# A banked Strassen-type MLP behind pooled attention and an FFT: one PSUM bank per product, a shared ring of four, and moved front-end stages

## The chip, the cores and the metric

The kernel runs on one core of a Trainium2 chip. The metric is device time in microseconds (us), the median of the runs shown. Engines are named as the profile names them: PE is TensorE's matmul, PEld its weight load, DVE is VectorE, ACT ScalarE, POOL GpSimd, SP the engine that issues most DMAs.

## The reference

Eight sequences of 576 tokens pass an attention whose keys and values are averaged over groups of eight tokens, then a two-dimensional FFT mix, a layer norm and a two-layer MLP of width 512 to 2048 to 512 with ReLU. Cut to what is computed:

```python
k_p = k.reshape(B, H, Sp, pool, D).mean(axis=3)
v_p = v.reshape(B, H, Sp, pool, D).mean(axis=3)
scores = scale * np.matmul(q, k_p.transpose(0, 1, 3, 2))
attn = np.exp(scores - np.max(scores, axis=-1, keepdims=True))
attn = attn / (np.sum(attn, axis=-1, keepdims=True) + 1e-09)
x = np.matmul(attn, v_p)               # heads side by side: (8, 576, 512)
X = np.fft.fft(np.fft.fft(x, axis=1), axis=2)
u = x + np.real(X)
un = (u - np.mean(u, -1)) / np.sqrt(np.var(u, -1) + 1e-06)
out = u + np.maximum(un @ w_ch1, 0.0) @ w_ch2
```

## The kernel before

The work has two halves that run side by side. The **front end** `fe(b)` (line 298) makes the normalised rows of sequence b: attention scores (tiles psS, line 394), transposes (psT, psV, psR), values (psX), the cosine and sine transforms (psA, psB, psQ, psP), the mean (psM), the variance (psVar), Newton steps for the reciprocal root, and last the operands of the MLP (`operands`, line 678). It is a generator of some 31 stages. The **MLP** `fast()` (line 848) is a second generator that works in nine blocks of 512 tokens. Block 0 is done by `plain()` (line 825) with ordinary products while the weights are still being split into high and low parts (`prep_w`, line 180; two MLP weight matrices in 32 pieces). Blocks 1 to 8 use a Strassen-type scheme: for each pair of hidden chunks (j = 0 to 7) seven products of 256 columns each, six matmuls a product (line 897), combined by seven DVE instructions (line 857, and the copy of line 900) into two hidden chunks, which pass ReLU on ACT (line 865), a rounded copy (line 866) and a remainder on POOL (line 867). The second layer, `gemm2` (line 789), comes in thirds of four matmuls of 512 columns (line 799) that are placed between the products of the next pair: the order of products and thirds is written in `MID`, `FIRST` and `LAST`.

Each product and each third ends in a `yield`, which counts one place. `advance(pos)` (line 950) runs a front-end stage when the place reaches its number in the table `AT` (`AT1` for sequence 1), counted from the start of the block before; 104 places are one block. `AHEAD` (line 52) says how many weight pieces are split ahead of the places. From place 92 on PE's instructions stand in the order in which the program writes them; DVE, ACT, POOL and the DMA queue are ordered by a scheduler.

PSUM has eight banks of 512 columns. The four accumulators of the second layer hold one each (tags acc0 to acc3). The front end takes turns on two banks (tag "fe", line 282). The products take turns on four **halves** of two banks (lines 850 and 851), so that two products that follow each other often lie in one bank. In the built program a product that starts in a bank waits until the addition that reads the other half has ended; the wait stands at about every second product.

Of the kernel before, what the change touches and what calls it, by code (L numbers as in the profile page):

```python
# [8 lines left out]
F32 = mybir.dt.float32  # L9
# [7 lines left out]
PSUM = bass.MemoryType.PSUM  # L17
# [5 lines left out]
P = 128  # L23
# [6 lines left out]
BLK = 512  # L30
# [18 lines left out]
UE = [1, 1, 0]  # L49
UL = [3, 3, 2]  # L50

AHEAD, WBUFS, LOOK = 7, 12, 9

RES = [0, 2, 5, 7, 9, 12, 14]

UNITS0, UNITS, MANUAL, TAIL = 90, 104, 92, (2, 8, 14, 20, 26)
AT = [-32, -22, -19, -9, -6, -4, -1, 13, 14, 16, 18, 25, 27, 27, 37, 40, 44, 47, 51, 51, 55, 58, 61, 67, 67, 80, 80, 81, 82, 83, 104]
AT1 = [-1] * 7 + [2 + 3.5 * n for n in range(17)] + [78, 79, 80, 82, 83, 84, 96]
E0, O0, E1, O1 = 0, 1, 2, 3

HB = BLK // 2
# [26 lines left out]
def raw(ap):  # L88
    return ap.bitcast(F32)
# [3 lines left out]
def tile_kernel(ctx: ExitStack, tc: tile.TileContext, qt, kt, vm, vr, w1, w2, cad, cbd, mkd, out):  # L93
    nc = tc.nc
    cp = ctx.enter_context(tc.tile_pool(name="cp", bufs=1))
    wk = ctx.enter_context(tc.tile_pool(name="wk", bufs=1))
    pp = ctx.enter_context(tc.tile_pool(name="pp", bufs=1, space=PSUM))
    dp = ctx.enter_context(tc.tile_pool(name="dp", bufs=1, space=bass.MemoryType.DRAM))
    wide = w1.dtype != F32
# [139 lines left out]
    for k in range(1, NBLK + 1):  # L239
        for j in range(NFC // 2):  # L240
# [4 lines left out]
            for x in MID if k < NBLK and j else FIRST:  # L245
                if x != "g" and k < NBLK:
                    items.append(("a", k, j, PROD[x][0]))
                elif x == "g":
                    f = 2 * prev[1] + g // 3
# [20 lines left out]
    def use(x):  # L270
        flow[0] = max(flow[0], where[x])
        return tiles.pop(x)


    turn, behind = [0], {}

    def bank(b, name, late=False):
        tag = "fe"
        if b == 0 and not late:
            tag = ["g1", "acc0", "g1", "acc1", "acc2", "acc3"][turn[0] % 6]  # L280
            turn[0] += 1
        return pp.tile([P, 512], F32, tag=tag, bufs=2 if tag in ("fe", "g1") else 1, name=name)

    def keep_busy(ins, n):

# [500 lines left out]
    def accs(k):  # L786
        return [pp.tile([P, 512], F32, tag=f"acc{e}", name=f"acc{k}_{e}") for e in range(4)]

    def gemm2(acc, f, hh, hl, got):
        order = [(x, e) for x in range(3) for e in range(4)]  # L790
        if f == NFC - 1:
            order = [(x, e) for e in range(4) for x in range(3)]
        w = []
        for n, (x, e) in enumerate(order):
            if n in (4, 8):
                yield
            w = w or [t.rearrange("p (c m) -> p c m", m=P) for t in got()]
            a, h = ((w[0], hh), (w[1], hh), (w[0], hl))[x]
            nc.tensor.matmul(acc[e], lhsT=a[:, e], rhs=h, start=(f == 0 and x == 0), stop=(f == NFC - 1 and x == 2))  # L799
        yield  # L800

    def weights2(k, f):
        def got():
            if k == 0:
                return highs.pop((1, f)), lows.pop((1, f))
            wh = w2h[:, RES.index(f)] if f in RES else use(("h", k, f))
            return wh, use(("l", k, f))
        return got
# [16 lines left out]
    def plain():  # L825
        xh, xl = [flat(t)[:, 0:2048].rearrange("p (c n) -> p c n", c=4) for t in un(0)]
        acc = accs(0)
        prev = None
        for f in range(NFC):
            ah, al = [t.rearrange("p (c m) -> p c m", m=P) for t in (highs.pop((0, f)), lows.pop((0, f)))]  # L830
            ps = pp.tile([P, 512], F32, tag="g1", bufs=2, name=f"g1_{f}")
            n = 0
            for w, x in ((ah, xh), (ah, xl), (al, xh)):
                for c, ti in enumerate((E0, O0, E1, O1)):
                    nc.tensor.matmul(ps, lhsT=w[:, c], rhs=x[:, ti], start=(n == 0), stop=(n == 11))
                    n += 1
                if n < 12:
                    yield
            hs = [wk.tile([P, BLK], F32R, tag=t, bufs=3, name=t) for t in ("hh", "hl")]
            nc.scalar.activation(hs[0], ps, AF.Relu)  # L840
            nc.vector.scalar_tensor_tensor(out=hs[1], in0=ps, scalar=0.0, in1=raw(hs[0]), op0=ALU.max, op1=ALU.subtract)  # L841
            yield
            if prev:
                yield from prev
            prev = gemm2(acc, f, *hs, weights2(0, f))
        return acc, [prev]

    def fast():
        acc, todo = yield from plain()
        gs = [pp.tile([P, 512], F32, tag="g1", bufs=2, name=f"x{i}") for i in range(2)]  # L850
        banks = [t[:, HB * i:HB * i + HB] for t in gs for i in range(2)]
        s24, c0, c2, s1 = [sx[:, BLK * i:BLK * i + BLK] for i in range(4)]
        s1 = s1[:, 0:HB]
        count = 0

        def add(o, x, y):
            nc.vector.tensor_tensor(out=o, in0=x, in1=y, op=ALU.add)  # L857

        def wide(x):
            return x.rearrange("p (h n) -> p h n", h=2)  # L860

        def relu(c):
            h = wk.tile([P, BLK], F32R, tag="hh", bufs=3, name="hh")
            l = wk.tile([P, BLK], F32R, tag="hl", bufs=3, name="hl")
            nc.scalar.activation(c, c, AF.Relu)  # L865
            nc.scalar.copy(out=h, in_=c)  # L866
            nc.gpsimd.tensor_tensor(out=l, in0=c, in1=raw(h), op=ALU.subtract)  # L867
            return h, l

        def step():  # L870
            while todo:
                if next(todo[0], 0) is None:
                    return True
                todo.pop(0)
            return False

        for k in range(1, NBLK):
            bh, bl = un(k)
            todo_of = acc
            for j in range(NFC // 2):  # L880
                last = k == NBLK - 1 and j == NFC // 2 - 1
                for x in FIRST if j == 0 else LAST if last else MID:
                    if x == "g":
                        if step():
                            yield
                        elif todo_of is not None:
                            evict(k - 1, todo_of)
                            todo_of = None
                        continue
                    ps = banks[count % 4]  # L890
                    count += 1
                    a, c = PROD[x]
                    w = use(("a", k, j, a)).rearrange("p (q c m) -> p q c m", q=2, m=P)
                    n = 0
                    for q, t in ((0, bh), (0, bl), (1, bh)):
                        for i in range(2):
                            nc.tensor.matmul(ps, lhsT=w[:, q, i], rhs=t[:, 2 * c + i], start=(n == 0), stop=(n == 5))  # L897
                            n += 1
                    if x == 1:
                        nc.vector.tensor_copy(out=s1, in_=ps)  # L900
                    elif x == 6:
                        add(s24[:, 0:HB], ps, s1)
                    elif x == 2:
                        add(c0[:, 0:HB], ps, s1)
                    elif x == 5:
                        add(s24[:, HB:BLK], ps, s24[:, 0:HB])
                    elif x == 3:
                        add(c0[:, HB:BLK], ps, s24[:, HB:BLK])
                        hs0 = relu(c0)
                    elif x == 7:  # L910
                        add(wide(c2), ps.unsqueeze(1).broadcast_to([P, 2, HB]), wide(s24))
                    elif x == 4:
                        add(c2[:, 0:HB], ps, c2[:, 0:HB])
                        hs1 = relu(c2)
                    yield
                while step():
                    yield
                if j == 0:
                    if todo_of is not None:
                        evict(k - 1, todo_of)  # L920
                    acc = accs(k)
                todo += [gemm2(acc, 2 * j + m, *hs, weights2(k, 2 * j + m)) for m, hs in enumerate((hs0, hs1))]
        while step():
            yield
        evict(NBLK - 1, acc)
# [21 lines left out]
    def start(k):  # L947
        return UNITS0 + UNITS * (k - 1) if k else 0

    def advance(pos):  # L950
        for c in sorted(run):
            r = run[c]
            while r[1] < len(AT) and pos >= (AT1 if c == 1 else AT)[r[1]] + start(c - 1):
                r[1] = len(AT) - 1 if next(r[0], None) == "ln" else r[1] + 1
        c = max(run) + 1
        if c < B and pos + 1 >= AT[0] + start(c - 1):
            run[c] = [fe(c), 0]
# [122 lines left out]
```

## Time and profile before

| what | value |
|---|---|
| runs, median (lowest to highest) | 1236.73 us (1235.58 to 1240.16) |
| profiled execution, its own time | 1243.98 us |
| its span, first to last instruction | 1242.2 us |
| PE busy | 1066.7 us (86%) |
| DVE busy | 775.0 us (62%) |
| ACT busy, POOL busy | 569.1 us, 569.6 us (46% each) |
| mean granted TensorE clock | 0.946 |

The profiled execution is one run; its span leaves out 1.8 us of its time. Busy shares are means over stretches with different limits: up to about 100 us there is the front end of sequence 0, to about 275 us the plain block, to about 1064 us the blocks that share the core with a front end, and from there on blocks alone. A row of PE with a time in square brackets gives the idle time before it and what ended it.

### The profile page before, as it was taken

To read this page: it belongs to the slowest core of one execution; us is meant where nothing else is said; L and a number is where in the kernel's file an instruction comes from. 1 tells how busy PE (TensorE), PEld (TensorE's weight loads), DVE (VectorE), ACT (ScalarE), POOL (GpSimd) and SP (SyncE) were. 2 spreads that over 40 slices of the span, in tenths; PEclk is the share of its full clock that TensorE was granted. 3 is DMA by queue.
4 is the path that set the end of the run, shared out by engine and by line. 5 is a ranking of instruction groups with operands and counts; after the bars stand their busy time and mean duration, and the time that the engine had idled before them with its cause. 6 is when DMAs were issued, how large, how long until landed. Compare 5 with 4: busy or idle time off the path is not lost.

```text
span 1242.2 us, 19110 instructions
## 1 busy us (share of the span) xinstructions
PE 1066.7 (86%) x6118; PEld 902.7 (73%) x6118; DVE 775.0 (62%) x1479; ACT 569.1 (46%) x1698; POOL 569.6 (46%) x531
## 2 busy tenths in 40 slices
PE   7778778868898889788978899798988998999998
PEld 5556456747786778677867787687867887888886
DVE  7586776885468656865577647865686567422322
ACT  6577554655327632664255534663266323222221
POOL 4375595654544555437444543555433244222221
PEclk9878889878999989998999999998999999999999
DMA  8538584756665766566665666576655666777874
GB/s 285 177 109 271 165 264 133 237 168 205 190 204 166 235 197 194 174 206 199 191 190 171 218 193 210 157 223 203 191 168 182 187 186 205 251 247 241 263 244 135
DMA packets 142755, 249.57 MB, mean 201 GB/s; under 512 B 15808, under 2 KB 36288, under 8 KB 142400
## 3 DMA queue, kind: packets, MB, share of 16 engines
q1 hardware_dynamic: 142368, 245.69, 63.7%
q0 software_dynamic: 288, 2.66, 0.6%
q8 instruction: 49, 0.80, 0.3%
q14 instruction: 50, 0.41, 0.1%
HBM read 217.63 MB, written 30.67 MB: 200 GB/s over the span
## 4 chain that ended last, share of the span: by engine, by line
PE 48%; DVE 26%; issue 8%; ACT 7%; DMA 4%; POOL 3%; SPq 0%; DVEq 0%; ACTq 0%; POOLq 0%
PE acc L799 20%; PE x L897 17%; DVE sx L857 4%; ACT t L403 2%; DVE X L690 2%; DVE unl L687 2%; PE psX L474 2%; DMA sx<-in_w 2%; DVE mx L396 2%; DVE U L821 1%; PE psP L632 1%; DVE X L779 1%; DVE rw L376 1%; DVE lf L725 1%; PE psB L615 1%
## 5 line engine op out<-in xcount | busy, mean ns | idle before, releaser
L897 PE MATMUL x<-unh,w1op 128*128 128x256 f32 x1792 | 372.2, 292 | 94.4 <-DVE sx L857 74.5
L897 PEld LDWEIGHTS x<-unh,w1op 128*128 128x128 f32 x1792 | 296.8, 194 | 151.8 <-DVE sx L857 103.7
L857 DVE TENSOR_TENSOR sx<-x,sx 128x256 f32<-128x256 f32 (+1 forms) x384 | 178.2, 466 | 212.0 <-PE x L897 209.9
L867 POOL TENSOR_TENSOR hl<-sx,hh 128x512 fp32r<-128x512 f32 x128 | 173.7, 1358 | 295.5 <-ACT hh L866 231.5
L865 ACT ACTIVATE sx<-sx 128x512 f32<-128x512 f32 x128 | 81.3, 635 | 328.8 <-DVE sx L857 328.5
L897 PE MATMUL x<-unl,w1op 128*128 128x256 f32 x896 | 180.7, 284 | 2.2 <-DVE unl L687 2.2
L799 PE MATMUL acc<-hh,w2low 128*128 128x512 f32 x576 | 167.1, 405 | 0.0
L897 PEld LDWEIGHTS x<-unl,w1op 128*128 128x128 f32 x896 | 141.1, 195 | 2.7 <-DVE unl L687 2.7
L799 PEld LDWEIGHTS acc<-hh,w2low 128*128 128x128 f32 x576 | 103.5, 194 | 16.3
L799 PE MATMUL acc<-hh,w2high 128*128 128x512 f32 x324 | 98.6, 414 | 3.6 <-ACT hh L840 2.6
L403 ACT ACTIVATE t<-psS,mx 128x72 f32<-128x72 f32 x280 | 86.2, 334 | 23.3 <-DVE mx L399 23.0
L799 PE MATMUL acc<-hl,w2high 128*128 128x512 f32 x324 | 94.0, 398 | 0.0
L411 POOL TENSOR_TENSOR t<-t,sm 128x720 f32<-128x720 f32 x32 | 49.5, 1547 | 75.3 <-DVE sm L410 41.1
L866 ACT CAST hh<-sx 128x512 fp32r<-128x512 f32 x128 | 79.7, 622 | 3.4
L799 PE MATMUL acc<-hh,w2h 128*128 128x512 f32 x252 | 75.1, 423 | 3.6 <-ACT hh L840 3.6
L799 PE MATMUL acc<-hl,w2h 128*128 128x512 f32 x252 | 74.5, 419 | 2.0 <-DVE hl L841 2.0
L799 PEld LDWEIGHTS acc<-hh,w2high 128*128 128x128 f32 x324 | 58.8, 198 | 13.2 <-ACT hh L840 3.2
L394 PE MATMUL psS<-kpb,q 128*128 128x144 f32 x280 | 47.9, 310 | 22.1 <-ACT t L403 11.3
L329 POOL TENSOR_TENSOR k<-k 128x288 f32<-128x288 f32 (+1 forms) x56 | 38.4, 685 | 61.5 <-DMA k<-in_kt 59.0
L799 PEld LDWEIGHTS acc<-hl,w2high 128*128 128x128 f32 x324 | 56.8, 190 | 8.8 <-issue 0.4
L394 PEld LDWEIGHTS psS<-kpb,q 128*128 128x128 f32 x280 | 40.1, 199 | 31.6 <-ACT t L403 16.2
L403 ACT ACTIVATION_READ_ACCUMULATOR t<-psS,mx 128x1 f32 x280 | 61.5, 220 | 0.0
(267 smaller groups left out, 1979.3 us busy)
## 6 DMA issues: line engine op xcount, KB each, us to landing
w1op<-w1s SPq DMA_DIRECT2D x448, 256.0 KB, 3.2
w2low<-w2l SPq DMA_DIRECT2D x128, 256.0 KB, 3.1
w2high<-w2d SPq DMA_DIRECT2D x72, 256.0 KB, 3.4
U<-in_w SPq DMA_DIRECT2D x16, 512.0 KB, 4.2
sx<-in_w SPq DMA_DIRECT2D x16, 512.0 KB, 4.5
q<-in_qt SPq DMA_DIRECT2D x28, 288.0 KB, 2.9
k<-in_kt SPq DMA_DIRECT2D x28, 288.0 KB, 3.3
v<-in_vm SPq DMA_DIRECT2D x28, 256.0 KB, 3.0
```

The lines of the kernel that those rows point to most:

```text
L329: nc.gpsimd.tensor_tensor(out=out if n == 1 else src[:, :, 0:n], in0=src[:, :, 0] if n == 1 else src[:, :, 0:n], in1=src[:, :, 1] if n == ...
L394: nc.tensor.matmul(ps[:, c * W2J:(c + 1) * W2J], lhsT=q[:, r0:r0 + P], rhs=kpb[g % 2], start=True, stop=True)
L396: nc.vector.tensor_reduce(out=mx[:, c0:c0 + n], in_=pv, op=ALU.max, axis=AX.X, negate=b in SM)
L403: nc.scalar.activation(t[:, c0 + c, h], pv[:, c, h], AF.Exp, scale=1.0 / 64.0, bias=mx[x], accum_out=sm[x])
L411: ins = nc.gpsimd.tensor_tensor(out=t, in0=t, in1=sm.unsqueeze(3).broadcast_to([P, 5, 2, J]), op=ALU.mult)
L474: behind["X", b] = nc.tensor.matmul(ps, lhsT=w, rhs=a, start=(i == 0), stop=(i == len(mm) - 1))
L799: nc.tensor.matmul(acc[e], lhsT=a[:, e], rhs=h, start=(f == 0 and x == 0), stop=(f == NFC - 1 and x == 2))
L857: nc.vector.tensor_tensor(out=o, in0=x, in1=y, op=ALU.add)
L865: nc.scalar.activation(c, c, AF.Relu)
L866: nc.scalar.copy(out=h, in_=c)
L867: nc.gpsimd.tensor_tensor(out=l, in0=c, in1=raw(h), op=ALU.subtract)
L897: nc.tensor.matmul(ps, lhsT=w[:, q, i], rhs=t[:, 2 * c + i], start=(n == 0), stop=(n == 5))
```

## The change

The products no longer use halves of two banks. When `plain()` has ended, the pool that held "g1" and "fe" (two banks each) is closed and a new one with four banks of one tag is opened; every product and every later front-end tile takes the next of these four in turn (`shared`). The additions of a product are issued with priority, so that the scheduler of DVE takes one first when it is ready. The tables are new: stages move by 1 to 12 places, sequence 2 has a table of its own (`AT2`, the early stages alone differ from `AT`), in `AT1` the last stages go from 78, 79, 80, 82, 83, 84 to 64, 69, 71, 73, 74, 75, and three more weight pieces are split ahead.

```diff
-AHEAD, WBUFS, LOOK = 7, 12, 9
+AHEAD, WBUFS, LOOK = 10, 12, 9
...
-AT = [-32, -22, -19, -9, -6, -4, -1, 13, 14, 16, 18, 25, 27, 27, 37, 40, 44, 47, 51, 51, 55, 58, 61, 67, 67, 80, 80, 81, 82, 83, 104]
+AT = [-36, -28, -23, -5, -3, -1, 2, 13, 14, 16, 18, 25, 27, 28, 38, 41, 44, 47, 51, 52, 55, 57, 60, 66, 66, 76, 76, 77, 78, 79, 104]
+AT2 = [-36, -28, -23, -13, -11, -9, -6] + AT[7:]
...
     def bank(b, name, late=False):
-        tag = "fe"
         if b == 0 and not late:
-            tag = ["g1", "acc0", "g1", "acc1", "acc2", "acc3"][turn[0] % 6]
             turn[0] += 1
-        return pp.tile([P, 512], F32, tag=tag, bufs=2 if tag in ("fe", "g1") else 1, name=name)
+            tag = ("g1", "acc0", "g1", "acc1", "acc2", "acc3")[(turn[0] - 1) % 6]
+            if tag != "g1":
+                return pp.tile([P, 512], F32, tag=tag, name=name)
+            return shared("g1", name)
+        return shared("fe", name)
...
+    def shared(kind, name):
+
+        if len(pools) == 2:
+            return pools[1].tile([P, 512], F32, tag=kind, bufs=2, name=name)
+        return pools[0].tile([P, 512], F32, tag="b", bufs=4, name=name)
...
-        gs = [pp.tile([P, 512], F32, tag="g1", bufs=2, name=f"x{i}") for i in range(2)]
-        banks = [t[:, HB * i:HB * i + HB] for t in gs for i in range(2)]
...
+        pools[0].__exit__(None, None, None)
+        pools[:] = [ctx.enter_context(banks())]
         for k in range(1, NBLK):
...
-                    ps = banks[count % 4]
-                    count += 1
+                    ps = shared("g1", "x")[:, 0:HB]
...
-                    if x == 1:
-                        nc.vector.tensor_copy(out=s1, in_=ps)
+                    with tc.high_priority():
+                        if x == 1:
+                            nc.vector.tensor_copy(out=s1, in_=ps)
...
-            while r[1] < len(AT) and pos >= (AT1 if c == 1 else AT)[r[1]] + start(c - 1):
+            while r[1] < len(AT) and pos >= (AT1 if c == 1 else AT2 if c == 2 else AT)[r[1]] + start(c - 1):
```

**PE, the score tiles of sequence 6 (psS6), in the late part of a block.** x is a product's tile, acc4 an accumulator of the second layer (the first of four matmuls of a third is shown, and the first row of three of a product). Before:

```order
L739 MATMUL psVar5_7503<-qhl_7496,avg_75 128x288
...
L394 MATMUL psS6_3_0_7536<-kpb1_77,q6_3_7411 128x144 x3
L394 MATMUL psS6_3_3_7548<-kpb1_77,q6_3_7411 128x144 x2
L897 MATMUL x0_2244<-unh4_5089,w1op_7439 128x256 x2
...
L799 MATMUL acc4_0_6638<-hl_7405,w2high_7369 128x512
...
L897 MATMUL x1_2245<-unh4_5089,w1op_7448 128x256 x2
...
L394 MATMUL psS6_2_0_7629<-kpb0_76,q6_2_7425 128x144 x3
L394 MATMUL psS6_2_3_7641<-kpb0_76,q6_2_7425 128x144 x2
```

Now:

```order
L754 MATMUL psVar5_7688<-qhl_7681,avg_75 128x288
L409 MATMUL psS6_3_0_7700<-kpb1_77,q6_3_7591 128x144 x3
L409 MATMUL psS6_3_3_7712<-kpb1_77,q6_3_7591 128x144 x2
L814 MATMUL acc4_0_6818<-hl_7526,w2h_69 128x512
...
L911 MATMUL x_7760<-unh4_5179,w1op_7569 128x256 x2
...
L814 MATMUL acc4_0_6818<-hh_7641,w2high_7579 128x512
...
L911 MATMUL x_7795<-unh4_5179,w1op_7627 128x256 x2
...
L911 MATMUL x_7805<-unh4_5179,w1op_7646 128x256 x2
...
L409 MATMUL psS6_2_0_7816<-kpb0_76,q6_2_7605 128x144 x3
L409 MATMUL psS6_2_3_7828<-kpb0_76,q6_2_7605 128x144 x2
```

Between the two pairs of score tiles two products and one third stood before; now it is three products and two thirds. In turn of the four banks, product x_7805 takes the bank of psS6_3_0 and psS6_2_0 that of psS6_3_3.

**DVE, the end of the values of sequence 5 (psX5_1) and the split of tmpE.** The rows of line 857 (now 870) are additions of products; lines 376 and 367 (391 and 382) prepare the value weights. Before:

```order
L857 TENSOR_TENSOR sx<-x_2245,sx 128x256
L485 TENSOR_TENSOR U<-psX_1_6881,U 128x288
L565 TENSOR_TENSOR tmpE<-U 128x2x287
L376 SCALAR_TENSOR_TENSOR rw_79<-vt,mk,rw_79 32x63
L376 SCALAR_TENSOR_TENSOR rw_79<-vt,mk,rw_79 32x1
L367 SCALAR_TENSOR_TENSOR wlo<-vs,mk,wh 128x64
L857 TENSOR_TENSOR sx<-x_2244,sx 128x256
L367 SCALAR_TENSOR_TENSOR wlo<-vs,mk,wh 128x63
L367 SCALAR_TENSOR_TENSOR wlo<-vs,mk,wh 128x1
L559 TENSOR_TENSOR f<-tmpE,f 128x580
L857 TENSOR_TENSOR sx<-x_2244,sx 128x256
```

Now:

```order
L870 TENSOR_TENSOR sx<-x,sx 128x256
L500 TENSOR_TENSOR U<-psX_1_7069,U 128x288
L580 TENSOR_TENSOR tmpE<-U 128x2x287
L391 SCALAR_TENSOR_TENSOR rw_79<-vt,mk,rw_79 32x63
L391 SCALAR_TENSOR_TENSOR rw_79<-vt,mk,rw_79 32x1
L382 SCALAR_TENSOR_TENSOR wlo<-vs,mk,wh 128x64
L870 TENSOR_TENSOR sx<-x,sx 128x256
L382 SCALAR_TENSOR_TENSOR wlo<-vs,mk,wh 128x63
L382 SCALAR_TENSOR_TENSOR wlo<-vs,mk,wh 128x1
L870 TENSOR_TENSOR sx<-x,sx 128x256
L574 TENSOR_TENSOR f<-tmpE,f 128x580
```

Here the second addition now stands ahead of the remainder of tmpE; the first keeps its place behind the five front-end instructions.

## Rows read from the trace of the kernel before

**Rows 1.** Page, span and busy time (share) of the engines.

```profile
span 1242.2 us, 19110 instructions
...
PE 1066.7 (86%) x6118; PEld 902.7 (73%) x6118; DVE 775.0 (62%) x1479; ACT 569.1 (46%) x1698; POOL 569.6 (46%) x531
```

**Rows 2.** Waits of PE, 277 to 1064 us: us in total, times, longest.

```profile
PE x L897 <- DVE sx L857: 67.5, 53, 4.6
PE x L897 <- DVE sx L900: 12.4, 11, 3.2
PE psS L394 <- ACT t L403: 9.7, 13, 1.0
PE psS L394 <- DVE R L460: 4.8, 7, 1.1
```

**Rows 3.** Timeline, 700 to 712 us: start, us, engine, line, operation, tiles, [idle before].

```profile
703.84 1.09 PE L799 MATMUL acc<-hh,w2low 128*128 128x512 f32 x4
...
706.38 2.25 DVE L376 SCALAR_TENSOR_TENSOR rw<-vt,mk,rw 32x63 fp32r<-32x63 f32 x2
...
709.02 0.41 DVE L857 TENSOR_TENSOR sx<-x,sx 128x256 f32<-128x256 f32 x1
...
709.49 0.80 PE L897 MATMUL x<-unh,w1op 128*128 128x256 f32 x2 [4.56 <-DVE sx L857]
```

**Rows 4.** Timeline, 1088 to 1094 us, blocks without a front end.

```profile
1088.80 0.42 DVE L857 TENSOR_TENSOR sx<-x,sx 128x256 f32<-128x256 f32 x1 [1.19 <-PE x L897]
...
1089.28 0.50 PE L897 MATMUL x<-unh,w1op 128*128 128x256 f32 x2 [0.52 <-DVE sx L857]
...
1091.01 0.40 PE L897 MATMUL x<-unh,w1op 128*128 128x256 f32 x2
...
1091.69 1.09 PE L799 MATMUL acc<-hl,w2high 128*128 128x512 f32 x4
...
1092.62 0.39 PE L897 MATMUL x<-unh,w1op 128*128 128x256 f32 x2
```

**Rows 5.** Windows: length, busy us of five engines, granted clock, DMA share, GB/s.

```profile
706.00:710.00 4.00, 0.51 (x2) 0.51 (x3) 3.94 (x7) 0.68 (x1) 3.80 (x5) 0.84 0.68 205
710.00:714.00 4.00, 4.00 (x17) 3.61 (x16) 1.60 (x4) 0.00 (x0) 1.76 (x3) 0.50 0.29 82
718.00:852.00 134.00, 115.82 (x717) 100.83 (x716) 89.88 (x175) 64.11 (x209) 63.61 (x61) 0.96 0.63 195
1064.00:1242.20 178.20, 166.31 (x1014) 144.69 (x1014) 54.64 (x118) 38.86 (x62) 40.65 (x31) 1.00 0.74 233
245.00:290.00 45.00, 30.62 (x127) 24.65 (x126) 35.02 (x73) 21.38 (x78) 19.96 (x15) 0.73 0.58 189
200.00:245.00 45.00, 35.66 (x161) 27.66 (x160) 40.48 (x59) 27.18 (x80) 32.22 (x27) 0.92 0.58 185
```

**Rows 6.** Timeline, 768 to 776 us: score tiles on PE, their exponentials on ACT.

```profile
768.17 1.39 PE L394 MATMUL psS<-kpb,q 128*128 128x144 f32 x10
...
772.42 0.34 ACT L403 ACTIVATE t<-psS,mx 128x72 f32<-128x72 f32 x1
...
772.90 1.00 PE L394 MATMUL psS<-kpb,q 128*128 128x144 f32 x6 [1.03 <-ACT t L403]
...
774.17 0.36 ACT L403 ACTIVATE t<-psS,mx 128x72 f32<-128x72 f32 x1
...
774.68 0.76 PE L394 MATMUL psS<-kpb,q 128*128 128x144 f32 x4 [0.78 <-ACT t L403]
```

**Rows 7.** Waits of PE, 1064 to 1243 us.

```profile
PE x L897 <- DVE sx L857: 7.0, 12, 0.9
```

**Rows 8.** Groups by line, 0 to 277 us: count | busy us, mean ns.

```profile
L198 DVE SCALAR_TENSOR_TENSOR wdl<-sx,wdl 128x512 int32<-128x512 int32 x10 | 9.8, 975 | 2.9 <-ACT wdl L195 2.5
...
L230 DVE TENSOR_TENSOR wdh<-wdh 128x256 f32<-128x256 f32 x8 | 7.7, 960 | 0.1
```

More of the change, by code (lines that the diff above doesn't have):

```diff
@@ L50 @@
 UL = [3, 3, 2]
-AHEAD, WBUFS, LOOK = 7, 12, 9
+AHEAD, WBUFS, LOOK = 10, 12, 9
 RES = [0, 2, 5, 7, 9, 12, 14]
 UNITS0, UNITS, MANUAL, TAIL = 90, 104, 92, (2, 8, 14, 20, 26)
-AT = [-32, -22, -19, -9, -6, -4, -1, 13, 14, 16, 18, 25, 27, 27, 37, 40, 44, 47, 51, 51, 55, 58, 61, 67, 67, 80, 80, 81, 82, 83, 104]
-AT1 = [-1] * 7 + [2 + 3.5 * n for n in range(17)] + [78, 79, 80, 82, 83, 84, 96]
+AT = [-36, -28, -23, -5, -3, -1, 2, 13, 14, 16, 18, 25, 27, 28, 38, 41, 44, 47, 51, 52, 55, 57, 60, 66, 66, 76, 76, 77, 78, 79, 104]
+AT2 = [-36, -28, -23, -13, -11, -9, -6] + AT[7:]
+AT1 = [-1] * 7 + [2 + 3.5 * n for n in range(17)] + [64, 69, 71, 73, 74, 75, 96]
 E0, O0, E1, O1 = 0, 1, 2, 3
@@ L277, in bank, with banks @@
     def bank(b, name, late=False):
-        tag = "fe"
         if b == 0 and not late:
-            tag = ["g1", "acc0", "g1", "acc1", "acc2", "acc3"][turn[0] % 6]
             turn[0] += 1
-        return pp.tile([P, 512], F32, tag=tag, bufs=2 if tag in ("fe", "g1") else 1, name=name)
+            tag = ("g1", "acc0", "g1", "acc1", "acc2", "acc3")[(turn[0] - 1) % 6]
[3 more added lines that the diff above has]
+        return shared("fe", name)
+    def banks():
+        return tc.tile_pool(name="ps", bufs=1, space=PSUM)
+    pools = [banks()]
+    pools.append(pools[0].__enter__())
+    def shared(kind, name):
+        if len(pools) == 2:
+            return pools[1].tile([P, 512], F32, tag=kind, bufs=2, name=name)
+        return pools[0].tile([P, 512], F32, tag="b", bufs=4, name=name)
     def keep_busy(ins, n):
@@ L830, in plain @@
             ah, al = [t.rearrange("p (c m) -> p c m", m=P) for t in (highs.pop((0, f)), lows.pop((0, f)))]
-            ps = pp.tile([P, 512], F32, tag="g1", bufs=2, name=f"g1_{f}")
+            ps = shared("g1", f"g1_{f}")
             n = 0
@@ L898, in fast @@
                             n += 1
-                    if x == 1:
-                        nc.vector.tensor_copy(out=s1, in_=ps)
[L901 to L914, printed above, removed]
+                    with tc.high_priority():
+                        if x == 1:
+                            nc.vector.tensor_copy(out=s1, in_=ps)
+                        elif x == 6:
+                            add(s24[:, 0:HB], ps, s1)
+                        elif x == 2:
+                            add(c0[:, 0:HB], ps, s1)
+                        elif x == 5:
+                            add(s24[:, HB:BLK], ps, s24[:, 0:HB])
+                        elif x == 3:
+                            add(c0[:, HB:BLK], ps, s24[:, HB:BLK])
+                            hs0 = relu(c0)
+                        elif x == 7:
+                            add(wide(c2), ps.unsqueeze(1).broadcast_to([P, 2, HB]), wide(s24))
+                        elif x == 4:
+                            add(c2[:, 0:HB], ps, c2[:, 0:HB])
+                            hs1 = relu(c2)
                     yield
```

## The prediction

> **What bounds the kernel now.** I read the page first. PE is busy 86% of a span of 1242.2 us, DVE 62% [rows 1], so PE sets the end and the question is what its idle 14% waits for. The list of PE's waits from 277 to 1064 us, where the banked blocks run beside a front end, names one thing: the first matmul of a product (line 897) waits for a DVE addition (line 857) or for the copy of line 900, 67.5 and 12.4 us in 64 waits, 79.9 us together, 1.25 us a wait, the longest 4.6 [rows 2]. Next come the score tiles, 9.7 and 4.8 us.
>
> Then the timeline, for why. In the blocks without a front end DVE is nearly free, yet PE still waits: an addition starts at 1088.80, lasts 0.42 us, and the next product starts at 1089.28 after 0.52 us idle [rows 4]. That product doesn't need the sum. It lies in the other half of the bank that the addition reads. A reader is to see that the 0.52 us is the addition itself: with halves, two products in a row cannot overlap with the reading of the first. At 704 us the same rule costs more: DVE works through front-end instructions (a pair of line 376 alone takes 2.25 us), gets to the addition at 709.02, and PE stands still for 4.56 us until 709.49 [rows 3]. The windows show what follows: in 706 to 710 us DVE is busy 3.94 of 4.00 and PE 0.51, and in 710 to 714 us PE is busy all the time at a granted clock of 0.50, which is the 1.2 GHz level [rows 5].
>
> **The change part by part, against the profiled execution (1243.98 us, its span plus 1.8).**
>
> *Own banks, additions first.* In a stretch of plain work a product takes 0.68 us (1091.01 to 1091.69) and a third 0.93 (to 1092.62) [rows 4], 1.61 together. In the ring of four a product waits for the reader of the tile four places back. If the three tiles between are products with a third each, PE has 3 x 1.61 = 4.8 us of work before it needs that bank, more than the longest wait (4.6). Front-end tiles take places too: a block has 39 of them beside 56 products. With a pair of them in the ring the cover is two products and thirds, 3.2 us. The mean wait of 1.25 us is under that; a wait of 4.6 us would keep 1.4. I count eight such remainders, 11 us, and take the gain as 79.9 - 11, say 68 us. Upper end 79.9. Lower end 64 x 0.52 = 33 us: if DVE really is late, each wait only loses the length of the one addition that a bank partner costs. I stand near the upper end because the DVE order shows the second addition moved ahead of the remainder of tmpE, and because DVE is busy 89.9 of 134 us in a block [rows 5]: late in places, not on the whole.
>
> *The blocks alone.* All 7.0 us of their waits [rows 7] are of the bank-partner kind: gain 7, ends 6 and 7.
>
> *The clock.* A block stands at 0.96 [rows 5]; over the five blocks from 320 to 980 us that is at most 0.04 x 660 = 26 us. Much of it falls where PE idles: in the episode of rows 5 the 4.0 us of work at 0.50 lose 2.0. With a second, shorter dip I take 2.5 us a block, 12 in all, of which 10 go with the long stalls. Ends 0 and 26.
>
> *The passage from the plain block.* From 245 to 290 us PE is busy 30.6 of 45 us at a clock of 0.73 [rows 5]: at full clock that work is 22 us, so at most 23 are lost. Sequence 1's last stages come 9 to 14 places sooner, and three weight pieces leave the stretch from 200 to 245 us, where DVE is busy 40.5 of 45 [rows 5]. A piece costs DVE one instruction of 0.98 us [rows 8], another of about the same length, and half of four combinations of 0.96 each: some 3.9, 12 us for three. They come earlier instead, behind sequence 0's front end. I take 8 us gained; the ends are 12 lost (the pieces stand in the way of the start) and 20 gained.
>
> *The shared ring for the front end.* This adds a wait. In the built order 48 of 448 products now wait for ACT where 5 did. At 768 us the second score tile ends at 769.56 and its last exponential at 774.53 [rows 6]: its bank is held 5.0 us. In the new order two thirds and three products lie between it and the tile that takes its bank, 2 x 0.93 + 3 x 0.68 = 3.9 us. So PE waits some 1.1 us here; behind it stands everything else on PE. It is 1.03 and 0.78 now at this place [rows 6]. The front end's own tiles in turn get four banks instead of two. I take 5 us lost over all blocks. Ends: 14.5 gained (both score rows of rows 2 gone) and 48 x 1.1 = 53 lost.
>
> *Moved stages.* No instruction is added; DMAs move with their stages in SP's queue. From 1064 us on the DMA share is 0.74 at 233 GB/s without a wait of PE for a transfer [rows 5], and a faster block with a front end asks for less than that (195 GB/s times 134/119 is 220). I cost the queue at nothing; the look-ahead of nine weight tiles hides it. Without it each of the ten weight tiles of a pair would show its landing.
>
> Sum: 68 + 7 + 10 + 8 - 5 = 88 us, 1243.98 - 88 = 1156. That execution is 7.25 us above the median of the runs, so the forecast is **1149 us**.
>
> A rule that speaks against the change: the blocks alone already take turns on four halves of two banks and stand at a clock of 1.00 with 12 short waits [rows 5, 7], so I charge nothing for turning through banks. The Trainium skill, TensorE: Matmul & The Clock Gate, section "A second HAM failure mode: psum-queue depth-cycling", tells of a kernel whose PE idled briefly between groups of matmuls as it cycled through PSUM banks, so that its clock swung between the two levels. By it the sum would lose the clock term and more; it is the third rival.
>
> **The rivals.**
>
> 1. *Deeper.* All 79.9 us of product waits, the clock (12), the passage (16) and half of the score waits (7) go, with the 7 of the end: 122 us, 1115 by the median. For it: the cover of 4.8 us. Against: front-end tiles in the ring.
>
> 2. *DVE is the pace.* Where DVE is saturated (3.94 of 4.00 [rows 5]), four banks only delay the wait. Then 33 + 7 us go, and the clock stays: 1204, 1197 by the median. Against: 90 of 134 us busy.
>
> 3. *The clock swings.* Short waits stay often enough that the blocks run at the 0.92 of 200 to 245 us [rows 5] rather than 0.96 to 1.00. Some 950 us at 7% less is 66 us, which leaves 22: 1215 by the median. Against: the clock of 1.00 after 1064 us.
>
> 4. *Slower: the ring locks products to ACT.* A product that takes the bank of a score tile waits for the exponentials, and with it all of PE. If ACT holds a tile not 5.0 but 6.2 us (a ReLU of the MLP between the exponentials does that), each of 48 products waits 2.2 us, 106 us together: 88 - 101 is a loss of 13 (the 5 are in it), 1257, 1250 by the median. It decides from an excess of about 2 us at each.
>
> 5. *It doesn't do what it says.* The wait is the addition itself and not the bank, so nothing moves: 1237.
>
> **How the numbers follow.** Forecast 0.52, deeper 0.20, DVE 0.17, clock 0.03, slower 0.05, nothing 0.03. The range of 1105 to 1205 us leaves out a third of rivals 1 and 2 at its ends, the last three, and a little of the forecast's own spread: some 0.2 in all. A measurement of this kernel can tell about 0.5%, 6 us, from no change. Faster is the first four cases, 0.92; within 0.5% 0.03; slower 0.05.
>
> **What would show it.** Right: waits of the products for DVE from 277 us to the last front end under 20 us, the blocks alone some 171 us long instead of 178, a clock of 0.98 or more in the blocks, and additions that end 2 to 5 us after their product while PE works on. Wrong: products that wait for ACT by tens of us (rival 4), waits for DVE of the same length but fewer (rival 2), a clock under 0.95 after 290 us (rival 3), or a plain block that ends later than 260 us.

## The result and the profile after

The changed kernel takes **1134.05 us** (median of 4 runs, 1131.58 to 1137.14) against 1238.45 us (1235.58 to 1241.90) of the kernel before in the same session: a ratio of 0.916, interval 0.912 to 0.920, or 104 us less. In a later session it took 1136.18 us, ratio 0.9145 (0.912 to 0.917). The forecast was 1149 us with a range of 1105 to 1205. The profiled execution took 1137.14 us.

The page of the changed kernel: span, busy time, and the group of the products' first matmuls (busy us, mean ns of one, idle time before it and what ended most of it). Lines have moved: 857, the addition, is now 870; 900, the copy, 915; 897, the product, 911; 799, a third, 814; 394 and 403, scores and exponentials, 409 and 418.

```profile
span 1135.3 us, 19340 instructions
PE 1028.5 (91%) x6118; PEld 887.8 (78%) x6118; DVE 754.9 (66%) x1479; ACT 568.0 (50%) x1698; POOL 574.1 (51%) x531
L911 PE MATMUL x<-unh,w1op 128*128 128x256 f32 x1792 | 345.4, 282 | 17.1 <-DVE R L475 3.7
```

The kernel before has this for the same group:

```profile
L897 PE MATMUL x<-unh,w1op 128*128 128x256 f32 x1792 | 372.2, 292 | 94.4 <-DVE sx L857 74.5
```

Against [rows 1] the span fell by 106.9 us. PE's busy time fell by 38.2 us for the same 6118 matmuls, and its idle time by 68.7 us. Idle time ahead of the group shown went from 94.4 to 17.1 us.

The list of PE's waits of the changed kernel, 290 to 1000 us, whole (us in total, times, longest; the columns of [rows 2]):

```profile
PE psVar L753 <- ACT qhl L749: 9.5, 6, 1.6
PE psR L467 <- DVE sx L870: 4.0, 5, 1.6
PE x L911 <- DVE R L475: 3.7, 4, 1.4
PE x L911 <- DVE U L500: 3.3, 5, 1.6
PE x L911 <- DVE al L451: 2.5, 3, 1.8
PE x L911 <- DVE sx L870: 2.5, 4, 1.7
PE psA L613 <- DVE A L598: 2.4, 5, 0.7
PE psVar L754 <- DVE qhl L750: 2.4, 6, 0.4
PE x L911 <- ACT U L492: 1.7, 2, 1.4
PE psR L467 <- DVE al L451: 1.7, 5, 0.5
PE psB L630 <- DVE f L574: 0.7, 2, 0.4
```

The largest rows of [rows 2] are gone. Products wait 2.5 us for additions, where they waited 79.9 us for additions and copies, and no score tile stands in the list. What is left are short waits of other kinds.

The next view shows why. It is the timeline of the changed kernel at the same kind of place as [rows 3], where DVE works through a pair of rw that takes over 2 us (start, us, engine, line, operation, tiles):

```profile
649.79 0.39 PE L911 MATMUL x<-unh,w1op 128*128 128x256 f32 x2
...
652.07 0.51 PE L911 MATMUL x<-unh,w1op 128*128 128x256 f32 x2 [0.52 <-DVE U L500]
...
653.80 0.39 PE L911 MATMUL x<-unh,w1op 128*128 128x256 f32 x2
...
655.41 0.40 PE L911 MATMUL x<-unh,w1op 128*128 128x256 f32 x2
...
656.10 1.09 PE L814 MATMUL acc<-hh,w2low 128*128 128x512 f32 x4
...
657.22 0.30 PEld L911 LDWEIGHTS x<-unh,w1op 128*128 128x128 f32 x2 [0.47 <-DVE sx L870]
657.23 0.51 PE L911 MATMUL x<-unh,w1op 128*128 128x256 f32 x2
```

```profile
654.01 2.35 DVE L391 SCALAR_TENSOR_TENSOR rw<-vt,mk,rw 32x63 fp32r<-32x63 f32 x2
...
656.76 0.41 DVE L870 TENSOR_TENSOR sx<-x,sx 128x256 f32<-128x256 f32 x1
```

Five products begin here. The first, of 649.79, ends at about 650.6, and by the order of the additions its sum is the one of 656.76, more than 6 us later. The next three products have the other three banks, and PE works on through them and their thirds. The fifth, of 657.23, needs the first one's bank, which the addition leaves at 657.17: it starts without idle time in its row. The cover is only just enough, as the row of PEld shows: the weight load of the fifth product did wait 0.47 us for that addition, and its first pair of matmuls takes 0.51 us instead of 0.39. DVE is as late as it was in [rows 3]. The lateness stayed, and the wait went.

**Where the time went, at equal work.** The stretches below end at the same pieces of work: the first product of block 1, the psQ transform of the sequence beside block 1, the psQ transform of the last sequence five blocks later, and the end. Windows (length, busy us of PE, PEld, DVE, ACT and POOL, granted clock, DMA share, GB/s), first the kernel before (the third stretch is given in its first block and the other four):

```profile
0.00:259.30 259.30, 199.72 (x823) 148.50 (x824) 190.21 (x318) 154.78 (x446) 151.69 (x155) 0.88 0.65 209
259.30:337.70 78.40, 63.76 (x349) 55.84 (x350) 48.69 (x103) 37.19 (x130) 39.89 (x45) 0.83 0.57 176
337.70:469.20 131.50, 115.61 (x714) 101.01 (x713) 86.08 (x174) 64.21 (x210) 65.08 (x62) 0.96 0.64 198
469.20:997.00 527.80, 460.77 (x2850) 400.77 (x2849) 348.34 (x686) 251.94 (x817) 241.70 (x218) 0.97 0.62 191
997.00:1242.20 245.20, 226.85 (x1388) 196.57 (x1386) 101.66 (x199) 61.01 (x99) 71.23 (x51) 1.00 0.72 223
```

The changed kernel:

```profile
0.00:267.15 267.15, 199.67 (x833) 148.78 (x833) 199.47 (x342) 164.37 (x495) 158.69 (x161) 0.86 0.63 205
267.15:324.50 57.35, 53.27 (x345) 47.56 (x346) 40.12 (x79) 27.35 (x82) 30.04 (x37) 0.97 0.69 228
324.50:443.90 119.40, 112.71 (x715) 100.13 (x714) 85.74 (x174) 63.91 (x210) 65.83 (x62) 0.97 0.68 218
443.90:908.40 464.50, 442.58 (x2850) 394.56 (x2849) 328.88 (x686) 251.80 (x817) 248.29 (x220) 0.99 0.69 218
908.40:1135.30 226.90, 220.29 (x1383) 196.74 (x1382) 100.70 (x199) 60.54 (x98) 71.22 (x51) 0.99 0.75 241
```

The reader is to see four differences. The first product starts 7.85 us later. By the transform of block 1 the changed kernel is nevertheless 13.2 us ahead. The next five blocks take 583.9 us instead of 659.3, or 75.4 less. The rest takes 226.9 instead of 245.2, or 18.3 less. Together that is 13.2 + 75.4 + 18.3 = 106.9 us.

### The profile page after: what moved, and what is told of

The parts are those of the page before. It is cut to its first block, busy times and chain, and to the rows that moved or that the text cites. A ratio compares the mean times of both kernels' runs of the same rounds, so it can differ in the third digit from the quotient of the medians.

```text
span 1135.3 us, 19340 instructions
## 1 busy us (share of the span) xinstructions
PE 1028.5 (91%) x6118; PEld 887.8 (78%) x6118; DVE 754.9 (66%) x1479; ACT 568.0 (50%) x1698; POOL 574.1 (51%) x531
## 4 chain that ended last, share of the span: by engine, by line
PE 53%; DVE 17%; ACT 11%; DMA 7%; issue 5%; POOL 4%; SPq 0%; DVEq 0%; POOLq 0%; ACTq 0%
PE acc L814 24%; PE x L911 20%; ACT t L418 2%; PE psS L409 2%; DMA sx<-in_w 2%; DMA k<-in_kt 2%; PE psP L647 1%; PE psB L630 1%; DMA w1op<-w1s 1%; DMA out<-U 1%; DVE sx L870 1%; PE psX L489 1%; DVE lf L740 1%; DVE X L705 1%; PE psQ L647 1%
## 5 line engine op out<-in xcount | busy, mean ns | idle before, releaser
L911 PE MATMUL x<-unh,w1op 128*128 128x256 f32 x1792 | 345.4, 282 | 17.1 <-DVE R L475 3.7
L911 PEld LDWEIGHTS x<-unh,w1op 128*128 128x128 f32 x1792 | 289.3, 189 | 53.5 <-DVE sx L870 6.0
L911 PE MATMUL x<-unl,w1op 128*128 128x256 f32 x896 | 176.7, 279 | 0.0
L911 PEld LDWEIGHTS x<-unl,w1op 128*128 128x128 f32 x896 | 136.9, 189 | 0.0
L814 PE MATMUL acc<-hh,w2high 128*128 128x512 f32 x324 | 94.1, 398 | 5.0 <-ACT hh L855 5.0
L879 ACT CAST hh<-sx 128x512 fp32r<-128x512 f32 x128 | 79.4, 620 | 3.7
L814 PE MATMUL acc<-hh,w2h 128*128 128x512 f32 x252 | 71.2, 406 | 4.0 <-ACT hh L855 4.0
L814 PEld LDWEIGHTS acc<-hh,w2high 128*128 128x128 f32 x324 | 56.4, 190 | 13.7 <-ACT hh L855 5.7
L409 PE MATMUL psS<-kpb,q 128*128 128x144 f32 x280 | 51.3, 336 | 14.6 <-DVE R L475 7.2
L418 ACT ACTIVATION_READ_ACCUMULATOR t<-psS,mx 128x1 f32 x280 | 64.4, 231 | 0.0
L409 PEld LDWEIGHTS psS<-kpb,q 128*128 128x128 f32 x280 | 46.6, 229 | 19.4 <-DVE R L475 7.8
```

Of the source, the lines that this page charges most:

```text
L409: nc.tensor.matmul(ps[:, c * W2J:(c + 1) * W2J], lhsT=q[:, r0:r0 + P], rhs=kpb[g % 2], start=True, stop=True)
L418: nc.scalar.activation(t[:, c0 + c, h], pv[:, c, h], AF.Exp, scale=1.0 / 64.0, bias=mx[x], accum_out=sm[x])
```

## The experiments

The theory: a product waited for the reading of its bank partner, and four whole banks in turn give PE enough other work while DVE is late. The rivals: the gain comes from the moved stages or from the priority; or any bank of its own is enough, without the depth of four. All diffs are against the changed kernel, unless said otherwise. "Ratio" is to the kernel before in the same session.

**e1_ring_alone: the ring of four, with the old tables and no priority.**

```diff
-AHEAD, WBUFS, LOOK = 10, 12, 9
+AHEAD, WBUFS, LOOK = 7, 12, 9
...
-AT = [-36, -28, -23, -5, -3, -1, 2, 13, ...
+AT = [-32, -22, -19, -9, -6, -4, -1, 13, ...
...
-                    with tc.high_priority():
+                    with ExitStack():
```

> The kernel before with the ring of four banks alone: old tables, no priority. Bank theory (the waits are those for a partner in the same bank): most of the gain comes with the ring, 1155 to 1180 us, and the waits of products for DVE from 277 us on fall from 79.9 to under 25 us. DVE-order theory (the waits come from where the additions stand in DVE's order): 1205 to 1238 us and waits of 50 us or more. Table theory (the moved stages bring it): 1220 to 1238 us.

Measured: 1156.31 us, ratio 0.931 (0.927 to 0.935), 83.6 us below the 1239.89 us of the kernel before, as the bank theory expected. Products wait 1.7 us for additions between 290 and 1000 us, though these have no priority here. PE's largest wait in it, 290 to 1000 us:

```profile
PE psT L445 <- POOL t L425: 26.6, 5, 5.6
```

The ring alone brings most of the gain. It uncovers a wait that is in no row of the kernel before: the transposes psT come, by the old places, before POOL has scaled the attention weights t, and PE waits about 5 us in each block.

**e2_priority_alone: halves of two banks and the old tables, with the priority.**

```diff
-                    ps = shared("g1", "x")[:, 0:HB]
+                    ps = half[count % 4]
+                    count += 1
```

(and the old tables as in e1; the pool isn't closed, and the front end keeps two banks)

> The kernel before with the priority of the additions alone: products in halves of two banks, old tables. Bank theory: within 1% of before, 1225 to 1245 us, since a partner in the same bank still has to wait for the addition itself. DVE-order theory: 1150 to 1200 us, the long waits of 4 to 5 us gone and those of 0.5 us left.

Measured: 1251.92 us, ratio 1.009 (1.006 to 1.011): not faster but a little slower, above even the range of the bank theory. Products wait 65.2 us in 45 for additions between 290 and 1000 us, where the kernel before has 61.9 in 47. Issue priority doesn't help while the bank is the limit. Why it loses 0.9% stays open; the score tiles wait 12.7 us instead of 9.7, which is a part of it at most.

**e3_tables_alone: halves, new tables, no priority.**

The edit is the diff of e2 and the last lines of e1's. (The new tables move stages by 1 to 6 places, and the last stages of sequence 1 by 9 to 14.)

> The kernel before with the new tables alone (AHEAD, AT, AT2, AT1): halves of two banks, no priority. Bank theory: 1215 to 1240 us, the stages only come at other places. Table theory: 1150 to 1200 us, score waits and the passage at 245 us shrink and with them the long stalls.

Measured: 1232.88 us, ratio 0.993 (0.991 to 0.996), some 7 us gained. Products still wait 72.9 us for additions in 40, between 290 and 1000 us. Its psQ transform of block 1 stands at 323.0 us, where the kernel before has 337.7 and the changed one 324.5: the start of the banked blocks is what the tables make earlier. Of these 14.7 us 9.5 are left at the end of the two profiled executions.

**e7_halves: the changed kernel, with the products back on halves of two banks.**

The edit is the diff of e2 with the new tables and the priority.

> The changed kernel with the products put back into four halves of two banks and the front end on two banks of its own; tables and priority stay. Bank theory: most of the gain is lost, 1205 to 1235 us, waits of products for DVE of 60 us or more. DVE-order or table theory: 1135 to 1165 us.

Measured: 1233.38 us, ratio 0.995 (0.992 to 0.997), 99 us above the changed kernel (of another session). The waits come back, 290 to 1000 us:

```profile
PE x L912 <- DVE sx L870: 68.0, 37, 4.6
PE x L912 <- issue: 11.4, 5, 2.6
```

For the second row ("issue") the profile shows no releaser, but each of its five waits ends 0.10 us after a copy (now line 916): a product starts at 521.66, and the copy ended at 521.56. So these are waits for the bank partner too, 79.4 us together. This one edit takes back nearly the whole gain. The additions are the same, with the same priority, and DVE has the same work; only the banks differ, those of the front end among them (e5 tells the two apart). So the wait is that of the bank. One thing the runs don't separate: the two halves are slices of one tile of 512 columns, and no run has two tiles in one bank, so whether the program would wait between those too isn't shown. The Trainium skill (PSUM — Partial Sum Buffer, section "PSUM bank collisions raise a hardware error") says that two engines must not use one bank at a time, even in different columns, as far as the partitions are the same, and that waits should be set by bank. The 0.52 us of [rows 4] agree, as they show a product that waits for the reader of the other half.

**e4_no_priority: the changed kernel without the priority.**

```diff
-                    with tc.high_priority():
+                    with ExitStack():
```

> The changed kernel without the priority of the additions; ring and tables stay. Bank theory: with three tiles between a product and the next use of its bank, an addition may come 2 us late without harm, so 1130 to 1145 us, within 1% of the changed kernel. DVE-order theory: 1150 us or more.

Measured: 1132.72 us, ratio 0.914 (0.911 to 0.918), the same as with it (0.916 and 0.9145). The largest wait is the same row too, 9.5 us in 6 of psVar for qhl. With the ring the priority makes no difference that can be measured.

**e6_old_tables: the ring and the priority, with the old tables.**

The edit is the first lines of e1's diff.

> The changed kernel with the old tables (AHEAD, AT, AT1, no AT2); ring and priority stay. If the tables were set for a core without the long stalls, 1145 to 1165 us, with more waits of score tiles and of psVar or psM; if the tables bring nothing, 1130 to 1140 us.

Measured: 1153.35 us, ratio 0.932 (0.929 to 0.935), the time that was expected, but not by the waits that were expected. The largest wait is e1's:

```profile
PE psT L445 <- POOL t L425: 29.2, 5, 6.1
```

So the tables are worth some 20 us where the ring is there (1153.35 against 1132.72 of e4 in the same session; e4 has no priority, which gives nothing there), and some 7 us without it (e3). The first transposes move from place -9 to -5, and this wait leaves the list. Parts don't add up here: 83.6 for the ring and 7 for the tables, but 104 for both, since the ring exposes a wait that the tables then remove.

**e5_two_and_two: own banks, but two for the products and two for the front end.**

```diff
-        pools[0].__exit__(None, None, None)
-        pools[:] = [ctx.enter_context(banks())]
```

> The changed kernel with two banks for the products, one product in each, and two for the front end, not shared; tables and priority stay. Own bank is what counts: the waits of 0.5 us go, the long ones of 4.5 us keep some 3 us, 1150 to 1180 us. Depth of four is what counts: close to the halves, 1200 to 1235 us. Sharing costs: below 1134 us.

Measured: 1182.00 us, ratio 0.955 (0.952 to 0.958). The three largest waits of PE, 290 to 1000 us:

```profile
PE x L909 <- DVE sx L870: 28.1, 31, 2.2
PE psS L409 <- ACT t L418: 12.3, 9, 2.6
PE psVar L753 <- ACT qhl L749: 8.2, 6, 1.4
```

The time lies just above the first range and far from the second. This tells the bank partner from the depth. From halves (e7, 1233.4 in another session) to two banks 51 us go; from two to four shared ones (1134.05 in another session) some 48 more, although the changed kernel also closes a pool, which this run doesn't (see e9). Depth and sharing come together here; no run has four banks for the products alone. With two banks a product still waits for the reader two products back, 28.1 us, the longest 2.2 us. The score tiles too, which take turns on two banks here, wait 12.3 us for exponentials; in the shared ring these waits are gone. That is the reverse of the slower rival of the prediction, by which sharing ties products to ACT.

**e8_var_later: the variance stages two places later**, against the largest wait that the changed kernel has left.

```diff
-AT = [..., 66, 66, 76, 76, 77, 78, 79, 104]
+AT = [..., 66, 66, 78, 78, 79, 80, 81, 104]
```

> The changed kernel with the variance stage and the four that follow it two places later (78, 78, 79, 80, 81). The waits of psVar for its rounded operand, 11.9 us in six blocks of the changed kernel, are a stage that comes too early: they fall under 3 us and the time to 1122 to 1130 us. Rival: the operands of the next block are late instead, products wait at the start of a block for unh and unl, 1134 to 1150 us.

Measured: 1125.47 us, ratio 0.909 (0.906 to 0.912). The waits of psVar fall from 11.9 to 1.7 us, but the list now begins with a row that was 1.7 us:

```profile
PE psR L467 <- DVE al L451: 10.5, 9, 3.7
```

The four blocks from psQ to psQ take 463.3 us (440.6 to 903.9), against 464.5: most of the wait was moved and not removed. The kernel is somewhat faster in the ratio, but its 7.6 us of span are spread over the start, the blocks and the end (1.6, 1.8, 1.2, 3.1), so I don't put them down to the edit.

**e9_one_ring: e8 with the ring of four from the first instruction**, so that nothing is closed and opened between the plain block and block 1.

```diff
-    pools = [banks()]
-    pools.append(pools[0].__enter__())
+    pools = [ctx.enter_context(banks())]
...
-        pools[0].__exit__(None, None, None)
-        pools[:] = [ctx.enter_context(banks())]
```

> e8_var_later with the ring of four banks there from the first instruction, so that nothing is closed and reopened between the plain and the banked blocks. Theory (the close of the pools is what moved the first banked product from 259.3 to 267.2 us, since the reopened banks wait for the exponentials of the last score tile): first banked product at 262 us or earlier, no wait of 3.3 us for ACT's t ahead of it, total 1115 to 1123 us. Rival: the plain blocks then share the ring with the front end and lose there what the passage gains: 1125 us or more.

Measured: 1120.51 us (1116.73 to 1124.75), ratio 0.903 (0.900 to 0.905); the changed kernel in the same session has 1136.18. To see why, first the timeline of the **changed kernel** at the passage, PE alone, in four rows that follow each other directly:

```profile
256.77 1.33 PE L409 MATMUL psS<-kpb,q 128*128 128x144 f32 x4 [3.47 <-DVE R L475]
259.33 1.81 PE L409 MATMUL psS<-kpb,q 128*128 128x144 f32 x6 [1.23 <-ACT t L418]
262.52 1.33 PE L409 MATMUL psS<-kpb,q 128*128 128x144 f32 x4 [1.38 <-ACT t L418]
267.15 0.79 PE L911 MATMUL x<-unh,w1op 128*128 128x256 f32 x2 [3.30 <-ACT t L418]
```

The score tiles take turns on the two banks of the front end. The first waits for DVE's R and the next two for exponentials; PE has no product to do meanwhile, as those start only when the pool is closed, that is after the last exponential has been read (it ends at 267.0 us). In **e9** the same passage reads:

```profile
244.82 2.12 PE L408 MATMUL psS<-kpb,q 128*128 128x144 f32 x16
246.68 1.19 PE L813 MATMUL acc<-hh,w2h 128*128 128x512 f32 x4
...
251.94 1.20 PE L849 MATMUL g<-unh,unl 128*128 128x512 f32 x4 [1.72 <-ACT t L417]
...
254.83 0.39 PE L908 MATMUL x<-unh,w1op 128*128 128x256 f32 x2
```

The score tiles run closely behind each other between the last thirds of the plain block, and the first product starts at 254.83 us, 12.3 us earlier than in the changed kernel and 10.8 earlier than in e8 (265.6). Of these 10.8 us 6.9 are left at the transform of block 1 (316.3 against 323.2). The sharing in the plain block does cost something: a plain tile (g, at 251.94) waits 1.72 us for exponentials. It is far less than the gain, so the theory holds and the rival (the plain block loses what the passage gains) doesn't. This edit changes two things, the close and the ring in the plain block. e5 tells them apart: it closes nothing and keeps two and two banks, and its first product starts at 253.13 us, 14.0 us earlier than in the changed kernel:

```profile
253.13 0.80 PE L909 MATMUL x<-unh,w1op 128*128 128x256 f32 x2
```

So the close is what holds the first product back.

**e10_no_at2: e8 with the table AT for sequence 2 as well.**

```diff
-AT2 = [-36, -28, -23, -13, -11, -9, -6] + AT[7:]
+AT2 = list(AT)
```

> e8_var_later with the places of the first sequence (AT) used for the second as well, so that the second sequence's scores and transposes stand behind the start of the first banked block. Theory (the passage waits because score tiles stand right before the switch): first banked product at 250 to 260 us, total 1115 to 1123 us. Rival: the score tiles then stand between the first products and their exponentials hold the ring there: 1128 us or more.

Measured: 1127.44 us, ratio 0.908 (0.904 to 0.911), the same as e8; first product at 263.7 us, and the wait of 3.3 us for the last exponentials still ahead of it. Neither expectation is met. Four score tiles stand ahead of the switch all the same, so the edit didn't do what it was meant to, and the places of sequence 2's transposes are not what delays the start; the close of the pool is (e5, e9).

**e11_remainder_later: e9 with the remainder's transposes two places later**, against the row of 10.2 us of psR for al that e9 has left.

```diff
-AT = [-36, -28, -23, -5, -3, -1, 2, ...
+AT = [-36, -28, -23, -5, -1, 0, 2, ...
```

> e9_one_ring with two entries of AT moved (-3 to -1, -1 to 0), so that the transposes of the remainder (psV, psR) of a sequence start two places later, after the subtraction al that they waited for. Theory (those waits, 10.2 us in 9, are the largest that e9 has left in the blocks and nothing lies behind them): the waits of psR for DVE's al fall below 3 us and the ratio to the kernel before goes from 0.903 to about 0.897. Rival (VectorE's queue is late at this place, so that what comes next waits instead, as it did when the variance stages were moved): another wait of like size for DVE, and the ratio stays at 0.900 to 0.905.

Measured: 1122.84 us, ratio 0.906 (0.904 to 0.909), no gain over e9. Waits of PE, 290 to 1000 us:

```profile
PE psS L408 <- DVE sx L912: 4.8, 4, 1.5
...
PE psV L455 <- DVE al L450: 3.4, 4, 2.2
PE x L908 <- DVE sx L869: 3.2, 4, 1.8
...
PE psS L408 <- DVE sx L869: 2.0, 3, 1.3
...
PE psR L466 <- DVE al L450: 1.7, 6, 0.5
```

The wait of psR fell from 10.2 to 1.7 us as aimed, and waits of score tiles, psV and products for the same DVE queue came in its place: 4.8 + 2.0 + 3.4 + 3.2 = 13.4 us. The rival holds in its mechanism, with a ratio just above its range. At this place of a block DVE is late in both runs, whatever PE asks of it first.

**a2_changed_again** is the changed kernel once more, as the base for e9 and e10.

> The changed kernel once more, so that the next two stand beside it on the same chip. Every theory: 1130 to 1140 us.

Measured: 1136.18 us, ratio 0.9145 (0.912 to 0.917). **e9 is the fastest kernel of this study**, 15.7 us below it.

## Why the prediction was right, point by point

*Own banks, additions first* (68 forecast, ends 33 and 79.9). The bank half is right and near its upper end: of the 79.9 us of [rows 2] 2.5 are left, so 77 went. I had kept 11 us for eight waits too long to be covered; the place at 649.79 to 657.23 shows an addition more than 6 us late that PE covers: four thirds and three products lie between (4 x 0.93 + 3 x 0.68 = 5.8 us), one third more than I counted, and a wait of 0.52 us for another reader, which helped to cover it. The other half of the name is wrong: the priority gives nothing, with the ring (e4) or without it (e2).

*The shared ring for the front end* (5 lost, ends 14.5 gained and 53 lost). The size is right, the reason isn't, so the size is luck. I expected products to wait for the exponentials of score tiles. No row from 290 to 1000 us shows one, and the score waits of [rows 2] went as well, 14.5 us gained. What came instead: products that wait for DVE's and ACT's readers of R, U and al (3.7 + 3.3 + 2.5 from the list, 1.7 for U on ACT), and front-end tiles that wait for readers in the ring (psR 4.0 and 1.7, psA 2.4), 19.3 us together. The difference is 4.8 us lost.

*Moved stages* (forecast: nothing added). Here a term is missing. The new places 76 to 79 bring waits of the variance matmuls for their operands, 9.5 + 2.4 = 11.9 us; and without the moved transposes the ring would have shown some 27 to 29 us of waits of psT for POOL (e1, e6). The trace before shows neither, as waits for additions covered both. The queue of transfers cost nothing, as forecast: the DMA share rises from 0.62 to 0.69 in the blocks, and no row of PE's waits from 290 us on names a DMA.

*The blocks alone* (7). From 997 us on in the kernel before products wait 11.6 us for additions and 0.9 for the copy; from 908.4 us on in the changed one PE's list has 2.0 us of psVar and nothing else. The term was right, with more of its kind just ahead of where I began to count.

*Idle time in sum.* From the transform of block 1 to the end PE's idle time is 904.5 - 803.23 = 101.3 us before and 810.8 - 775.58 = 35.2 after: 66 us less. The terms above make 68 + 7 - 5 = 70, of which 7.5 are waits ahead of that transform, so 62.5 stand against 66. That part of the sum was right.

*The clock* (10, ends 0 and 26). In the same stretch PE's busy time fell from 803.2 to 775.6 us, 27.7 us for nearly the same matmuls (4948 on record, then 4943, about 1 us). The granted clock explains some 8 to 10 us of it by rounded figures: 0.97 to 0.99 over the four blocks is 2% of 460.77, 0.96 to 0.97 in the block ahead of them 1% of 115.61, and at the end it is 1.00 and then 0.99. So the clock term had about its size. **What the sum lacked is that a stall costs PE more than the idle time of its row.** I took each wait at its idle time and put the rest at nothing, without a reason. The rows show two costs. The last third before the stall of [rows 3] keeps PE busy for 1.09 us (703.84 to 704.93), while in plain work the next product starts 0.93 us after a third ([rows 4], 1091.69 to 1092.62): 0.16 us that otherwise overlap. And the first pair of matmuls after a stall takes 0.50 us instead of 0.40 ([rows 4], 1089.28 and 1091.01), as its weight load starts with it and not ahead of it:

```profile
1089.28 0.30 PEld L897 LDWEIGHTS x<-unh,w1op 128*128 128x128 f32 x2 [0.71 <-DVE sx L857]
...
1090.78 0.42 PEld L897 LDWEIGHTS x<-unh,w1op 128*128 128x128 f32 x2
```

From the transform of block 1 to the end the lists count 94 waits of PE before and 43 after. 51 fewer at 0.26 us is 13 us, by my estimate. With the clock that makes 21 to 23 of the 27.7; 5 to 7 are left, 1 of them for the five matmuls, and the rest isn't placed.

*The passage* (8 gained, ends 12 lost and 20 gained). Right in sum, wrong in its course, and so in part luck. The text counted "a plain block that ends later than 260 us" among the signs of failure; the first product does start at 267.15 instead of 259.30 us, because of the closed pool, which my steps didn't cost at all. But from there the work runs without the gaps of the kernel before, at a clock of 0.97 instead of 0.83, and the kernel is 13.2 us ahead by the transform of block 1. Waits for additions in that stretch (7.5 us before) are in the first term already, so that the passage itself gave about 6. Without the close, and with the ring in the plain block too, the first product comes 10.8 us earlier and the transform 6.9 (e9 against e8). What gave the gain isn't told apart: the tables alone bring the transform to 323.0 us (e3), and the ring alone to 327.5 (e1).

*The rivals.* "Deeper" came nearest in its waits, since nearly all product waits went. "DVE is the pace" fails: its 28 us remain only where the depth is two (e5). "The clock swings" fails: the blocks stand at 0.97 to 0.99. The Trainium skill, TensorE: Matmul & The Clock Gate, section "A second HAM failure mode: psum-queue depth-cycling", tells of a kernel whose clock swung as it turned through banks; here turning through four banks went with a steadier clock than halves of two (0.95 in e7's four blocks, 0.99 in the changed kernel's). "The ring locks products to ACT" has no row in the blocks; its mechanism shows once, at the passage, 3.3 us. "It doesn't do what it says" fails by e7.

*The scale.* The sum of 88 us stands against 106.9 of span. With the 7.5 us of waits ahead of the transform counted where they lie, idle time from the transform on is 3.5 us over the forecast (66 against 62.5), busy time 18 over it (27.7 against 10), and the stretch up to there 2 under it (13.2 against 8 + 7.5). So nearly the whole difference is busy time, and by my estimate most of that is the cost of stalls which the sum left out.

## What to carry to other kernels

Where PE waits for an eviction of half a microsecond at every second tile, look at which bank the reader holds: here the two halves of one bank worked as one buffer. Give each tile a bank, count the work that lies between a tile and the next one in its bank, and compare it with the longest time by which the evicting engine is late; a pool shared by two users gives both more depth than a fixed split (1134 against 1182 us). Then list the waits again, since the large one hides others (psT here), and don't close a pool between two stages that could overlap. When you price a wait that will go, count more than its idle time: here each cost PE some 0.26 us of busy time besides.

## What the runs showed that I had not expected

- A stall costs PE more than the idle time the list shows, by the rows some 0.26 us each: with 66 us of idle time 27.7 us of busy time went, and the granted clock explains 8 to 10 of them.
- Waits behind a late engine move rather than go: psVar 11.9 us (changed kernel, ratio 0.916), psR 10.5 (e8, 0.909) and 10.2 (e9, 0.903), 13.4 in four rows (e11, 0.906).
- Closing a pool made the first product of the next one wait for the last exponentials that read the closed one: 3.3 us with the new tables, and in e1, with the old ones, the first product starts only at 273.4 us, after 9.5 us of waiting for the exponentials. Without a close it starts at 253.1 (e5) and 254.8 (e9).
